# Two tokens in the two halves of the one-hot rows

## The chip, the core and the metric

The kernel runs on one core of a Trainium2 chip. The metric is the device time of the whole program in microseconds (us), taken as the median of several executions. Before the change it is 1927.19 us, from three runs between 1919.88 and 1936.14 us. One further execution was recorded by the hardware profiler; all rows below come from it.

The engines are called as in the profile: PE is TensorE's matrix multiply, PEld its weight load, DVE is VectorE, ACT is ScalarE, POOL is GpSimd and SP is SyncE, which issues DMAs.

## What is computed

The output is `x + A(xn) + B(xn)`, with `xn` the layer norm of x (2048 tokens, 512 wide).

- A is attention with 32 heads of width 16 that share one key and one value head, followed by an output projection.
- B is a mixture of 4096 tiny experts. For each of 32 heads a token has scores against 64 + 64 half keys; the two best of each give four candidate pairs, and the two best of those four are two experts with softmax gates. An expert is a row of `u` and a row of `v`: its contribution is `gate * gelu(xn . u) * v`. So a token uses 64 (head, choice) slots.

```
out = einsum("nhk,nhk,nhkd->nd", g, act, ve)     # g: gates, act: gelu(xn . u[e]), ve: v[e]
```

## The kernel before

The tokens are 16 tiles of 128, in four groups of 512. The kernel is one long list of 256 **attention steps** (`att_steps`), written out in order for every engine. A step issues, for TensorE, two score products, eight products with the values, two more score products (L327, L341, L327), and on ScalarE four exponentials of 128x1024 (L330). Behind these, in `fill`, each step pulls work for the expert part from a generator (`score_thread`). Every piece of it yields a cost (in units of about a microsecond; a 512-wide matmul counts `UNIT = 0.235`); `spent` adds these up, and step d of 256 pulls pieces until `spent` reaches a straight line that ends at `FILL = 948`, or until 4.0 units (`MOST`) are pulled in this step. So the costs that are yielded decide in which step a piece comes, and not how long it takes.

For the groups 0 and 1 (phases with `ph < NSP`) the experts' rows are gathered from HBM by indirect DMA on POOL (L976), and DVE forms a dot product (L988) and an update (L1023) for each of 512 gathered tiles. These are spread over the steps by `pos`, which advances per step by a number that depends on the stage (1.4 in the stage that the change touches, `dense_on[0] == 2`).

For the groups 2 and 3 the experts are computed **densely**: all 4096 rows of `u` are multiplied with the group (`pact`, L733), the result is multiplied with a dense matrix of gates (4096 experts by 512 tokens), and then by all of `v` (`pout`, L861). The change is in how that **matrix of gates** is made, once per dense group, so twice in the program:

1. `batch` writes for each token its 64 slots: two index numbers per slot (df1: 0 to 127, df2: 0 to 31, which together name one of 4096 experts), on POOL (L635, L638), and its gate, on DVE, as a float16 part and a remainder (L648, L649). The index is written twice, once for the gate's high part and once for its remainder, so a token has 128 numbers per array: rows 0 to 63 with the high gates, rows 64 to 127 with the remainders.
2. `spread` (L758) transposes the arrays on TensorE, so that the 128 rows lie on the partitions and the tokens along the row, and ScalarE copies each out of PSUM as float16 (L759).
3. `onehot(q)` builds, for 16 tokens, on DVE, `oa` (128 rows x 128 numbers x 16 tokens, 1 where the number is the row's index, L783), `ob` (128 x 32 x 16, the same for the second index, L785) and multiplies `ob` by the gates (L786). It is called two pieces ahead.
4. For each token one matmul `pg` (L815): `oa`'s 128x128 slice of this token is loaded as weights, `ob`'s 128x32 slice is streamed through. The sum over the 128 rows adds each slot's high part and remainder at its expert's place. Sixteen tokens fill one PSUM bank (128 x 512).
5. `copies` (L820) brings the bank to SBUF by two ScalarE copies of 128x256; every fourth piece, 64 tokens are written to HBM by SP's queue (L825, L827). The copies of a piece are issued before the next piece of the generator, or in the middle of the next attention step.

```
oa, ob = OH.pop(q)
p = xtile("pg")
for i in range(TB):
    nc.tensor.matmul(p[:, i * NB:(i + 1) * NB], oa[:, :, i], ob[:, :, i], start=True, stop=True)
...
yield 2.0
```

There are 32 such pieces (`NQ`) of 16 tokens (`TB`) in a dense group. `xtile` takes one of three PSUM banks that all short products share; the scores have four banks of their own, and L341's product one. The one-hot tiles come from a pool of eight tiles (`wk`) that the float32r halves of `u` and `v` use too.

## Time and profile before

| | us |
|---|---|
| median of 3 runs | 1927.19 |
| lowest and highest | 1919.88, 1936.14 |
| the profiled execution | 1931.19 |
| its span on the core | 1929.5 |
| PE busy | 1865.4 (97%) |
| DVE busy | 1633.0 (85%) |
| ACT busy | 1294.3 (67%) |
| POOL busy | 693.5 (36%) |

The span is the time from the first to the last instruction, and busy is the time in which an engine had at least one instruction in work. TensorE's clock is granted in stretches; the page gives it as a share of full speed, and its mean over the execution is 0.98. In the answers of the trace, "x32" is a count of instructions, "128*128" the rows and columns of the array that a matmul or weight load takes, and an arrow names what an engine waited for.

The two stretches with `pg` matmuls begin at 609 us and at 1417 us of the span.

### The profile page before, as it was taken

The numbers are of one execution on the slowest core, as the hardware profiler recorded it, in microseconds if no ns is written. First come the engines' busy times: TensorE is split into PE (matmuls) and PEld (weight loads), VectorE is DVE, ScalarE is ACT, GpSimd is POOL, SyncE is SP. The second block draws the span as 40 slices with busy tenths as digits, with TensorE's granted clock in tenths as the row PEclk, the third lists the DMA queues.
The fourth block names the chain that finished last, engine by engine and source line by source line (L and its number), as shares of the span: only waits on it lengthen the run. The fifth ranks groups of instructions, "written<-read, shape, count | busy, mean of one in ns | idle before, by whom it ended". The sixth has DMA issues, their size and how long they took to land.

```text
span 1929.5 us, 35007 instructions
## 1 busy us (share of the span) xinstructions
PE 1865.4 (97%) x10990; PEld 995.2 (52%) x10990; DVE 1633.0 (85%) x6381; ACT 1294.3 (67%) x1803; POOL 693.5 (36%) x920
## 2 busy tenths in 40 slices
PE   6879999999999999999999999999999999999998
PEld 4544444555555544555555454555555555555553
DVE  6626788889998976999999897899988879999994
ACT  3336666655557887877877555555578877888873
POOL 1202334334453213343444354344522124344430
PEclk9989999999999989999999999999999999999999
DMA  7856878887673668799889977877645778899882
GB/s 269 300 202 229 291 263 294 287 294 277 231 268 121 216 213 260 248 283 292 267 288 308 353 278 241 295 243 264 216 138 194 267 222 291 271 284 284 283 274 83
DMA packets 245724, 491.14 MB, mean 255 GB/s; under 512 B 93972, under 2 KB 106260, under 8 KB 245532
## 3 DMA queue, kind: packets, MB, share of 16 engines
q0 software_dynamic: 73728, 268.47, 41.4%
q1 hardware_dynamic: 170568, 219.56, 34.9%
q8 instruction: 88, 1.44, 0.3%
q10 hardware_dynamic: 1236, 0.82, 0.1%
q14 instruction: 104, 0.85, 0.1%
HBM read 427.41 MB, written 56.07 MB: 251 GB/s over the span
## 4 chain that ended last, share of the span: by engine, by line
PE 84%; DVE 3%; ACT 2%; issue 1%; DMA 1%; another core or an unknown queue 0%; SPq 0%; ACTq 0%; DVEq 0%
PE pv L341 23%; PE psc L531 18%; PE sc L327 17%; PE pact L733 10%; PE pout L861 9%; PE pg L815 2%; PE pwo L434 2%; ACT pt L330 2%; PE pw L487 2%; DVE oh L783 1%; DMA wk<-dw 1%; DVE xa L1023 1%; DMA wqt<-in_wqT_dram 0%; PE pwt L494 0%; PE pwl L409 0%
## 5 line engine op out<-in xcount | busy, mean ns | idle before, releaser
L330 ACT ACTIVATE pt<-sc 128x1024 f32<-128x1024 f32 x1024 | 994.4, 1026 | 459.2 <-PE sc L327 405.9
L976 POOL DMA_INDIRECT g<-in_uv_dram,idx x512 | 555.0, 1084 | 1009.5 <-DVE xa L1023 531.9
L341 PE MATMUL pv<-pt,vaug 128*32 128x512 f32 x4096 | 508.9, 615 | 0.0
L531 PE MATMUL psc<-wk,xt 128*128 128x512 f32 x1536 | 390.9, 402 | 6.6 <-DVE wk L497 3.5
L327 PE MATMUL sc<-qa,kaug 64*128 64x512 f32 x2048 | 387.0, 453 | 7.7 <-ACT pt L330 6.9
L1023 DVE SCALAR_TENSOR_TENSOR xa<-g,w,xa 128x512 f32<-128x512 f32 x512 | 371.5, 744 | 0.1
L988 DVE CUSTOM_DVE_ANT_0 g<-g,xa 128x512 f32<-128x512 f32 x512 | 335.2, 680 | 6.6 <-DMA g<-in_uv_dram,idx 6.6
L531 PEld LDWEIGHTS psc<-wk,xt 128*128 128x128 f32 x1536 | 279.4, 189 | 110.5 <-issue 40.3
L327 PEld LDWEIGHTS sc<-qa,kaug 64*128 64x128 f32 x2048 | 157.1, 187 | 326.1 <-ACT pt L330 194.3
L341 PEld LDWEIGHTS pv<-pt,vaug 128*32 128x32 f32 x4096 | 108.8, 111 | 255.7 <-issue 254.1
L546 DVE FIND_INDEX8 i<-m,psc 128x8 uint32<-128x64 f32 x1024 | 206.2, 220 | 0.0
L733 PE MATMUL pact<-xt,wk 128*128 128x512 f32 x768 | 196.0, 400 | 0.0
L861 PE MATMUL pout<-wk,wd 128*128 128x512 f32 x768 | 194.9, 402 | 0.2 <-DVE wd L919 0.2
L544 DVE MAX8 m<-psc 128x8 f32<-128x64 f32 x1024 | 146.1, 213 | 41.2 <-PE psc L531 40.0
L861 PEld LDWEIGHTS pout<-wk,wd 128*128 128x128 f32 x768 | 140.8, 188 | 47.4 <-issue 5.5
L733 PEld LDWEIGHTS pact<-xt,wk 128*128 128x128 f32 x768 | 139.4, 188 | 48.6 <-issue 17.9
L864 DVE TENSOR_TENSOR da<-da,pout 128x512 f32<-128x512 f32 x128 | 82.7, 678 | 10.1 <-PE pout L861 8.6
L698 DVE TENSOR_TENSOR wk<-rw,wk 128x512 fp32r<-128x512 f32 x128 | 84.7, 682 | 7.1 <-ACT wk L697 7.1
L783 DVE TENSOR_TENSOR oh<-oh 128x2048 f16<-128x2048 f16 x64 | 78.0, 1219 | 2.3 <-PE pg L815 1.7
L815 PEld LDWEIGHTS <-oh 128*128 128x128 f16 x1024 | 68.4, 163 | 13.6 <-issue 4.8
L815 PE MATMUL pg<-oh 128*128 128x32 f16 x1024 | 73.7, 246 | 0.8 <-DVE oh L786 0.7
L697 ACT CAST wk<-rw 128x512 fp32r<-128x512 f32 x128 | 74.0, 632 | 0.0
(159 smaller groups left out, 1356.4 us busy)
## 6 DMA issues: line engine op xcount, KB each, us to landing
wk<-dw SPq DMA_DIRECT2D x96, 512.0 KB
wqt<-in_wqT_dram SPq DMA_DIRECT2D x32, 512.0 KB
dw<-wk SPq DMA_DIRECT2D x32, 512.0 KB
rw<-in_ub_dram SPq DMA_DIRECT2D x64, 256.0 KB
rw<-in_vb_dram SPq DMA_DIRECT2D x64, 256.0 KB
gy<-dg SPq DMA_DIRECT2D x64, 256.0 KB
qa<-dqh SPq DMA_DIRECT2D x128, 64.0 KB
g<-in_uv_dram,idx POOLq DMA_INDIRECT x512
```

The lines of the kernel that those rows point to most:

```text
L327: nc.tensor.matmul(p[:, b, :], kaug[o:o + 64, kc * P:(kc + 1) * P], QA[u][o:o + 64, i, :], start=True, stop=True)
L330: nc.scalar.activation(pt, p, AF.Exp, scale=SCALE)
L341: nc.tensor.matmul(PV[u][32 * j:32 * j + 32, :], vaug[:, kc, :], pt[:, b, :], start=kc == 0, stop=kc == 15)
L531: nc.tensor.matmul(p, XT[k][:, a, j * P:(j + 1) * P], WC[n_][k][:, bb, :], start=n == 0, stop=n == 11)
L544: nc.vector.max(m8[:, jb, s, :], p[:, s * E:(s + 1) * E])
L546: nc.vector.max_index(i8[:, jb, s, :], m8[:, jb, s, :], p[:, s * E:(s + 1) * E])
L733: nc.tensor.matmul(p, us[:, a, k * P:(k + 1) * P], XT[k][:, c, :], start=n == 0, stop=n == 11)
L815: nc.tensor.matmul(p[:, i * NB:(i + 1) * NB], oa[:, :, i], ob[:, :, i], start=True, stop=True)
L861: nc.tensor.matmul(p, wd[0][:, a, j * P:(j + 1) * P], vs[:, c, :], start=n == 0, stop=n == 5)
L976: nc.gpsimd.indirect_dma_start(out=gt, out_offset=None, in_=uv, in_offset=bass.IndirectOffsetOnAxis(ap=IDX[ph, c, ti][:, s:s + 1], axis=0))
L988: nc.vector.tensor_tensor_reduce(u, u, XN[TPH * ph + ti], scale=1.0, scalar=0.0, op0=OP.mult, op1=OP.add, accum_out=a[:, i:i + 1])
L1023: nc.vector.scalar_tensor_tensor(acc, v, w[:, i:i + 1], acc, op0=OP.mult, op1=OP.add)
```

## The change

A one-hot tile now serves 32 tokens instead of 16: rows 0 to 63 hold the 64 slots of an even token, rows 64 to 127 those of the odd token behind it. A token then has 64 rows, so one matmul can no longer sum high parts and remainders; two matmuls of 64 rows each do it one behind the other into the same place (`start=r == 0, stop=r == 1`), with the same weights. `ob` comes in two versions, times high gates and times remainders.

What follows from it in the code:

- `batch` writes the indices once; the four arrays (df1, df2, high gates, remainders) are one tile of the pool `da` where they were three halves of two tiles.
- `spread` runs four times instead of three, and takes from each array and 128-token block the even and the odd tokens by two products with every second column of the identity (64 columns each), in place of a transpose of 128 columns. Its copy is 128x256 in place of 128x512.
- `onehot` is called one piece ahead instead of two; a piece has one `oa` for 32 tokens, one comparison for `ob` and two multiplications.
- `pg` goes to two PSUM banks per piece, one for the even tokens, one for the odd ones; four copies per piece put the tokens back in order, so they write every second element.
- A piece yields 3.6 instead of 2.0; there are 16 instead of 32 per group. `FILL` goes from 948 to 935. The loads that hang on piece numbers (`later_split` and what follows) are moved to the pieces with about the same tokens.

```diff
-FILL = 948.0
+FILL = 935.0
 ...
     def dense_tiles():
-        for _ in range(2):
-            da = big.tile([P, 2, D], F32, name="da", tag="da", bufs=2)
-            for i in range(2):
-                DT.append(da[:, i, :].rearrange("p (t r s) -> p t r s", t=GT, r=2))
+        da = big.tile([P, 4, GT, 64], F32, name="da", tag="da", bufs=2)
+        DT.extend(da[:, i] for i in range(4))
...
-        for r in range(2):
-            G_.tensor_add(df2[:, :, r, w], hi, ii[:, 1])
+        G_.tensor_add(df2[:, :, w], hi, ii[:, 1])
...
-            V.tensor_copy(dgt[:, :, 0, w], gh)
-            stt(dgt[:, :, 1, w], gg, GS, gh, op0=OP.mult, op1=OP.subtract)
+            V.tensor_copy(dgh[:, :, w], gh)
+            stt(dgl[:, :, w], gg, GS, gh, op0=OP.mult, op1=OP.subtract)
...
-        NQ = 512 // TB
+        NQ = 512 // (2 * TB)
...
             for j in range(GT):
-                nc.tensor.transpose(p[:, j * P:(j + 1) * P], DT[n][:, j].rearrange("p r s -> p (r s)"), ident)
-            nc.scalar.copy(tr[:, n, :], p)
+                for h in range(2):
+                    nc.tensor.matmul(p[64 * h:64 * h + 64, 64 * j:64 * j + 64], DT[n][:, j, :], ident[:, h::2],
+                                     start=True, stop=True)
+            nc.scalar.copy(tr[:, n, :], p[:, :256])
...
                 oa = kt(F16, (P, P, TB))
                 nc.vector.tensor_tensor(out=oa, in0=io, in1=bc(0, tb, P), op=OP.is_equal)
-                ob = obs[:, q % 3]
-                nc.vector.tensor_tensor(out=ob, in0=io[:, :NB, :], in1=bc(1, tb, NB), op=OP.is_equal)
-                nc.vector.tensor_mul(ob, ob, bc(2, tb, NB))
+                ob = obs[:, q % 2]
+                nc.vector.tensor_tensor(out=ob[:, 1], in0=io[:, :NB, :], in1=bc(1, tb, NB), op=OP.is_equal)
+                for i in range(2):
+                    nc.vector.tensor_mul(ob[:, i], ob[:, 1], bc(2 + i, tb, NB))
...
-            onehot(q + 2)
+            onehot(q + 1)
             oa, ob = OH.pop(q)
-            p = xtile("pg")
+            ps_ = [xtile("pg") for _ in range(2)]
             for i in range(TB):
-                nc.tensor.matmul(p[:, i * NB:(i + 1) * NB], oa[:, :, i], ob[:, :, i], start=True, stop=True)
+                for r in range(2):
+                    for h in range(2):
+                        o = slice(64 * h, 64 * h + 64)
+                        nc.tensor.matmul(ps_[h][:, i * NB:(i + 1) * NB], oa[o, :, i], ob[o, r, :, i],
+                                         start=r == 0, stop=r == 1)
...
-                for hb in range(2):
-                    nc.scalar.copy(st[hb][:, :, ql * TB:(ql + 1) * TB], pv_[:, 16 * hb:16 * hb + 16, :])
-                if ql == 3:
+                for h in range(2):
+                    pb = ps_[h].rearrange("p (t b) -> p b t", b=NB)
+                    for hb in range(2):
+                        to = st[hb][:, :, ql * 2 * TB:(ql + 1) * 2 * TB].rearrange("p b (t h) -> p b t h", h=2)
+                        nc.scalar.copy(to[:, :, :, h], pb[:, 16 * hb:16 * hb + 16, :])
+                if ql == 1:
...
-            yield 2.0
+            yield 3.6
```

More of the change, by code (lines that the diff above doesn't have):

```diff
@@ L623, in batch @@
             dense_tiles()
-        df1, df2, dgt = DT[:3]
+        df1, df2, dgh, dgl = DT
         ii = T("ii", F32, [P, 2, BT, 8])
@@ L633, in batch @@
         G_.tensor_scalar(hi, ii[:, 1], 32.0, -32.0, op0=OP.is_ge, op1=OP.mult)
-        for r in range(2):
-            G_.tensor_add(df2[:, :, r, w], hi, ii[:, 1])
+        G_.tensor_add(df2[:, :, w], hi, ii[:, 1])
         G_.tensor_scalar(hi, hi, -2.0, None, op0=OP.mult)
-        for r in range(2):
-            G_.tensor_add(df1[:, :, r, w], hi, ii[:, 0])
+        G_.tensor_add(df1[:, :, w], hi, ii[:, 0])
         def gates():
@@ L726, in dense @@
         yield 0.0
-        df1, df2, dgt = DT[:3]
         def activations(b, us, p):
@@ L757, in spread @@
             for j in range(GT):
-                nc.tensor.transpose(p[:, j * P:(j + 1) * P], DT[n][:, j].rearrange("p r s -> p (r s)"), ident)
-            nc.scalar.copy(tr[:, n, :], p)
+                for h in range(2):
+                    nc.tensor.matmul(p[64 * h:64 * h + 64, 64 * j:64 * j + 64], DT[n][:, j, :], ident[:, h::2],
+                                     start=True, stop=True)
+            nc.scalar.copy(tr[:, n, :], p[:, :256])
         io = kt(F16, (P, P, TB))
         nc.sync.dma_start(io, d_io)
-        tr = kt(F16, (P, 3, 512))
+        tr = kt(F16, (P, 4, 256))
         hh = late[0].tile([P, 2, 512], F32, name="gy", tag="gy", bufs=3)
@@ L772, in dense @@
             yield None
-        spread(2)
-        yield 0.45
+        for n in (2, 3):
+            spread(n)
+            yield 0.45
         dense_on[0] = 2
@@ L801, in load_totals, with copies @@
                     LIVE.add(t)
-        obs = kt(F16, (P, 3, NB, TB))
+        obs = kt(F16, (P, 2, 2, NB, TB))
         onehot(0)
         yield from rest_of_first
-        onehot(1)
         for q in range(NQ):
-            t0, ql = q // 4 * 64, q % 4
+            t0, ql = q // 2 * 64, q % 2
             if ql == 0:
                 st = [late[0].tile([P, 16, 64], F32, name="gst", tag="wd", bufs=4) for _ in range(2)]
-            onehot(q + 2)
+            onehot(q + 1)
             oa, ob = OH.pop(q)
-            p = xtile("pg")
+            ps_ = [xtile("pg") for _ in range(2)]
             for i in range(TB):
-                nc.tensor.matmul(p[:, i * NB:(i + 1) * NB], oa[:, :, i], ob[:, :, i], start=True, stop=True)
-            pv_ = p.rearrange("p (t b) -> p b t", b=NB)
-            def copies(pv_=pv_, st=st, ql=ql, t0=t0):
-                for hb in range(2):
-                    nc.scalar.copy(st[hb][:, :, ql * TB:(ql + 1) * TB], pv_[:, 16 * hb:16 * hb + 16, :])
-                if ql == 3:
+                for r in range(2):
[3 more added lines that the diff above has]
+                                         start=r == 0, stop=r == 1)
+            def copies(ps_=ps_, st=st, ql=ql, t0=t0):
+                for h in range(2):
[4 more added lines that the diff above has]
+                if ql == 1:
                     def part(b0, b1, st=st, t0=t0):
@@ L834, in dense @@
             POST.append((copies, lambda: None))
-            if q in (NQ - 16, NQ - 12):
-                later_split((NQ - 16, NQ - 12).index(q))
-            if q == NQ - 3:
+            if q in (NQ - 8, NQ - 6):
+                later_split((NQ - 8, NQ - 6).index(q))
+            if q == NQ - 2:
                 on_act(lambda: halves.__setitem__(2, half_split(2, 0)))
-            if q == NQ - 3:
+            if q == NQ - 2:
                 quiet[0] = 3
-            if q == NQ - 2:
+            if q == NQ - 1:
                 dense_on[0] = 3
@@ L845, in dense @@
                 later_split(2)
-            if q == NQ - 1:
                 later_split(3)
-            yield 2.0
+            yield 3.6
         held, ready, used = [], [], [0]
```

## The prediction

> **What bounds the kernel now.** First the page: which engine is full, and where along the span that is otherwise.

> ```profile
> PE 1865.4 (97%) x10990; PEld 995.2 (52%) x10990; DVE 1633.0 (85%) x6381; ACT 1294.3 (67%) x1803; POOL 693.5 (36%) x920
> ...
> PE   6879999999999999999999999999999999999998
> ...
> DVE  6626788889998976999999897899988879999994
> ...
> PEclk9989999999999989999999999999999999999999
> ...
> PE 84%; DVE 3%; ACT 2%; issue 1%; DMA 1%; another core or an unknown queue 0%; SPq 0%; ACTq 0%; DVEq 0%
> ```

> PE is full nearly everywhere and carries 84% of the chain that ended last; the kernel's time is a sum of PE work. DVE has slices that are as full. So the next view is by stretch: the two in which `pg` is made, then single attention steps of the first.

> ```profile
> 609.47:716.75 107.28, 105.84 (x951) 55.38 (x950) 97.50 (x201) 91.90 (x153) 21.48 (x18) 0.90 0.64 205
> 1417.71:1528.33 110.62, 105.18 (x964) 56.78 (x963) 99.94 (x203) 93.04 (x154) 26.33 (x23) 0.92 0.60 199
> ```

> ```profile
> 615.21:620.56 5.35, 5.35 (x60) 3.10 (x58) 5.21 (x14) 4.92 (x9) 0.00 (x0) 1.00 0.08 21
> ...
> 684.54:691.60 7.06, 7.06 (x60) 3.35 (x58) 6.38 (x14) 5.20 (x10) 1.15 (x1) 0.76 0.84 263
> ...
> 666.70:671.50 4.80, 4.62 (x43) 2.19 (x42) 4.70 (x11) 4.29 (x9) 1.95 (x2) 1.00 0.98 260
> ```

> The columns are: length, busy time of PE, PEld, DVE, ACT, POOL, granted clock, DMA share, GB/s. The two stretches take 107.28 + 110.62 = 217.9 us, 36 steps. A step with two pieces (32 tokens) takes 5.35 us, with PE at 5.35, DVE at 5.21 and ACT at 4.92: three engines are close together, PE ahead. The same step takes 7.06 us where the clock was 0.76. A step with one piece (16 tokens) takes 4.80 us.

> The low clock has a pattern, shown by windows of 3.41 us, the length of the clock's stretches here:

> ```profile
> 681.79:685.20 3.41, 3.41 (x40) 2.59 (x38) 3.38 (x7) 2.55 (x5) 2.13 (x2) 1.00 0.80 238
> 685.20:688.62 3.42, 3.42 (x18) 0.60 (x16) 3.32 (x10) 2.43 (x4) 1.15 (x1) 0.50 0.71 254
> 702.27:705.68 3.41, 3.41 (x46) 2.48 (x38) 2.37 (x6) 2.78 (x5) 2.01 (x2) 1.00 0.81 233
> 705.68:709.10 3.42, 3.42 (x27) 1.21 (x28) 3.39 (x9) 3.42 (x8) 0.91 (x1) 1.00 0.94 328
> ```

> A window that holds a whole burst of 32 `pg` (40 PE instructions) is followed by one at half clock; the third row holds such a burst too and is not. From the mean clocks 0.90 and 0.92 the stretches lose 0.10 x 107.28 + 0.08 x 110.62 = 19.6 us, and a cold window costs 7.06 - 5.35 = 1.71 us: some 11 to 12 of them.

> **The change, part by part.** *The matmuls.* What decides is the pace of `pg`:

> ```profile
> 646.62 2.13 PEld L815 LDWEIGHTS <-oh 128*128 128x128 f16 x32 [0.36 <-DVE xa L1023]
> ...
> 643.68 0.19 PEld L327 LDWEIGHTS sc<-qa,kaug 64*128 64x128 f32 x2 [0.61 <-ACT pt L330]
> 643.68 0.49 PE L327 MATMUL sc<-qa,kaug 64*128 64x512 f32 x2 [0.31 <-ACT pt L330]
> ...
> L327 PEld LDWEIGHTS sc<-qa,kaug x2048: 182/183/335, 140.2 to 1910.0; 64*128 64x128 f32 x187
> L327 PE MATMUL sc<-qa,kaug x2048: 383/492/793, 140.2 to 1910.3; 64*128 64x512 f32 x187
> ...
> L815 PEld LDWEIGHTS <-oh x1024: 141/166/182, 613.0 to 1528.1; 128*128 128x128 f16 x171
> ...
> 649.51 0.16 PEld L341 LDWEIGHTS pv<-pt,vaug 128*32 128x32 f32 x8 [0.36 <-issue]
> ```

> (Where a row has three durations, they are the least, the median and the greatest, in ns.) Thirty-two weight loads, each with its matmul, take 2.13 us, 66.6 ns a pair. The change doubles their number: 64 for 32 tokens. Each has 64 rows, and rows 0 to 63 and 64 to 127 alternate. The trace holds exactly this form: the scores (L327) use 64 rows, alternating, into two banks. Two of their loads together took 0.19 us where one takes 183 ns, two matmuls together 0.49 us where one takes 492 ns. So two halves of the array load and multiply at the same time, started within 10 ns. From that I take one pair of halves at 66.6 ns, 33.3 ns per matmul: 64 take 2.13 us again, the change in `pg` is **0**. The bounds: 33.3 ns, or no overlap, 66.6 ns, which would add 1024 x 66.6 ns = +68 us. I take the low end because the nearest rows, of the same shape of array, show two at the price of one. The instructions would then come at four per 66.6 ns, 17 ns each; the L341 row has eight loads in 0.16 us, so out of PE's own queue it can start that fast, in short runs.

> *Attention around them.* The built program has one piece of 32 tokens in each of 16 consecutive steps per group, where it had 14 steps of 32 and 4 of 16. So the 36 steps become 32; four steps' attention goes to other stages with as much other work as before, and costs PE there what it cost here. The yielded costs fall by 32 x 2.0 - 16 x 3.6 = 6.4 per group, less 0.45 for the fourth `spread`, 11.9 in all, and the line's end by 13, so the rest of the work keeps its steps nearly. What goes is the surplus of the 8 one-piece steps: 4.80 us against (5.35 - 2.13) + 1.07 = 4.29 us, 8 x 0.51 = **-4 us**.

> *DVE.* Its rows of the first stretch, with ACT's, and the waits of the `pg` loads over the whole span (microseconds, times):

> ```profile
> L783 DVE TENSOR_TENSOR oh<-oh 128x2048 f16<-128x2048 f16 x31 | 37.8, 1219 | 1.7 <-PE pg L815 1.7
> ...
> L820 ACT COPY gst<-pg 128x256 f32<-128x256 f32 x64 | 21.6, 411 | 0.2 <-PE pg L815 0.2
> ...
> L786 DVE TENSOR_TENSOR oh<-oh 128x512 f16<-128x512 f16 x32 | 13.6, 425 | 1.2
> L785 DVE TENSOR_TENSOR oh<-oh 128x512 f16<-128x512 f16 x31 | 12.9, 417 | 0.0
> ```

> ```profile
>   DVE oh L785: 3.3, 9
>   DVE oh L786: 2.5, 6
>   DVE xa L1023: 1.3, 4
>   DVE oh L783: 0.7, 2
> ```

> For 32 tokens DVE now does 2 x (1219 + 417 + 425) = 4122 ns and will do 1219 + 417 + 2 x 425 = 2486 ns: 1.64 us less, 52 us over 32 pieces. Nearly all of it lies beside PE and is worth nothing. What is worth something is PE's wait for the one-hot tiles, 3.3 + 2.5 + 0.7 + 1.3 = 7.8 us; the first piece of a group still waits, and part of each wait is PE's own switch, so **-5 us**, between 0 and -8. The call one piece ahead instead of two is covered: a piece is one step, its 2.5 us are issued ahead of the step's updates, and the 5.35 us of a step hide them; without that cover it would be 2.5 us a step. POOL's saved adds are nothing, as no wait names them.

> *ACT.* Copies per 32 tokens stay four of 128x256, 411 ns each by their row. That they write every second element is not in the trace; I take no difference, between 0 and +0.4 us each if the write takes twice as long, which beyond the 5.35 - 4.92 = 0.43 us of slack would add up to 1.2 us a step, 38 us. All four now stand behind each other between the second and third exponential, where two stood. By a step's rows (ACT 4.92 of 5.35) the round still closes; nothing.

> *PSUM.* Two of the three banks per piece, freed in the middle of the next step, as two pieces did before: nothing. *DMAs:* the same writes of 64 tokens, the same loads at the same tokens; SP's queue passes nothing new: nothing.

> *The transposes.*

> ```profile
> 1420.89 1.09 PE L758 MATMUL ptd<-ident,da 128*128 128x128 f32 x8
> 1423.30 0.66 PE L758 MATMUL ptd<-ident,da 128*128 128x128 f32 x4 [1.31 <-ACT oh L759]
> ```

> Eight take 1.09 us, 136 ns each, 24 in all 3.3 us. The 64 new ones have half the columns: at half the price 4.4 us, at the full one 8.7 us, and between halves of the array that overlap 2.2 us. I take +1 us, between -1 and +5. The wait of 1.31 us stays.

> *The switch of the array.* Behind the burst at 646.62 the loads end at 648.75, and the next score's load starts at 648.85; such a pause of about 0.1 us stands on either side of a burst. If it comes from going between 128 and 64 rows, it goes: 32 x 2 x 0.1 = -6 us; if not, 0. I take -2. [...]

> *Cold windows.* Bursts keep their length of 2.13 us and come once per step; I take the same 19.6 us: 0.

> Sum: 0 - 4 - 5 + 1 - 2 = **-10 us**. Against the profiled execution, 1931.19 us, that gives 1921; that execution is 4 us above the median of the runs shown, and from the median it gives 1917. I predict 1919 us. By 1%, 19 us, is about what a measurement of this kernel tells from no change; the forecast lies within it. Its own range is 1908 to 1931 us.

> **The rivals.**

> *No overlap (slower).* The two halves could take turns, since their weight loads come every 33 ns and no row shows float16 loads of 64 rows. Halving the rows does not halve a load: the 64-row load of the scores takes 183 ns, the 128-row float16 one 166 ns (medians). Then 64 matmuls take 4.26 us and a step 7.48 us: +68 us, and a burst longer than a window of 3.41 us leaves nearly every step a cold window: 32 x 1.71 = 55 us against 19.6, +35 at most. 1977 to 2022 us, about 1995. It decides from some 48 ns per matmul on, where 2048 x 15 ns make 30 us and the time is 1% above before. Against it: the rows of the scores.

> *PE is fed too slowly (slower).* The bursts now are never faster than 66.6 ns per load and matmul; if its sequencer can hand over no more than that, and a queue holds some 16 of them ready when a burst starts (my assumption; no row gives its depth), then of 64 the first 32 run at 33 ns, in the time in which 16 more arrive, and the last 32 at 66.6: 32 x 1.07 = +34 us, 1953 us. For it speaks that no longer run in the trace is faster. [...]

> *Locked cold windows (slower).* Four steps in a row from 677.45 to 705.59 us took about 7.06 us, close to two windows of 3.41 us: once a burst falls into a window, the next one falls there as well. So far the one-piece steps broke this. Without them all 32 could lock: 55 us against 19.6, 1919 + 35 = 1954 us.

> *No cold windows (faster).* If matmuls in both halves count as more work for whatever grants the clock, the 19.6 us go: 1899 us.

> *DVE never cost anything.* Its waits turn into ACT's, and it stays at 1924 to 1931 us; this lies in the forecast's range.

> **How the numbers follow.** Forecast with the last rival 0.53, no overlap 0.18, fed too slowly 0.11, locked 0.08, no cold windows 0.10. Range: from 1897, with the fast case, to 1965, with the two middle ones; left out is the case of no overlap, 0.18. Faster by over 1% (below 1908): 0.10 + 0.03 = 0.13. Slower by over 1% (above 1946): 0.18 + 0.08 of the fed one + 0.06 of the locked one = 0.32. Within: 0.55.

> **What would show it.** In the profile after, a burst of 64 weight loads of 64 rows takes 2.1 us if the forecast holds, 2.9 to 3.2 us if fed too slowly, 4.3 us without overlap. Steps of the stretch at full clock take 5.1 to 5.4 us, DVE falls to about 1580 us busy, and hardly a wait of `pg` for the one-hot tiles is left but the first of a group. The stretches' clock near 0.91 means that the cold windows are as before; near 0.76 that they are locked. The prediction is wrong if the burst is longer than 2.5 us, or if ACT's copies take over 0.6 us.

## The result, and the profile after

The changed kernel takes 1950.11 us (median of 11 runs, 1941.72 to 1956.99), the kernel before beside it 1928.37 us (11 runs): ratio **1.0108**, 95% interval 1.0085 to 1.0131. It is slower by 1.1%, 22 us. The forecast was 1919 us and "no change that can be told"; the time is 31 us above it, though inside the stated range of 1897 to 1965 us.

The same program was measured again on three chips, numbered 5, 6 and 10, always beside the kernel before; the record does not name the chip of the first measurement. Since the outcome depends on the chip, the table has each; everything below compares runs of one chip, or ratios. A "pause" is idle time of TensorE within a burst, the run of `pg` matmuls of one piece, for which the profile names no releaser.

| | ratio to before | interval | pauses in `pg` bursts |
|---|---|---|---|
| first measurement | 1.0108 | 1.0085 to 1.0131 | yes |
| `after_4` (chip 5) | 1.0103 | 1.0071 to 1.0135 | yes |
| `after_again` (chip 6) | 1.0035 | 1.0009 to 1.0060 | no |
| `after_3` (chip 10) | 1.0022 | 1.0000 to 1.0044 | no |

So there are two questions: why the kernel gained nothing anywhere, and what costs another 0.7 to 0.8% where the bursts pause. The page of the kernel after, with the groups of `pg` and the two queues of the kind "instruction":

```profile
PE 1868.2 (96%) x12118; PEld 998.4 (51%) x12118; DVE 1586.8 (81%) x6317; ACT 1294.8 (66%) x1805; POOL 679.0 (35%) x888
...
q8 instruction: 97, 1.59, 0.3%
...
q14 instruction: 102, 0.84, 0.1%
...
L816 PE MATMUL pg<-oh 64*128 64x32 f16 x2048 | 79.2, 245 | 6.8 <-issue 5.2
L816 PEld LDWEIGHTS <-oh 64*128 64x128 f16 x2048 | 72.0, 157 | 18.8 <-issue 16.5
```

The profiled execution took 1952.04 us, its span 1950.2 us. PE's busy time hardly moved (1865.4 to 1868.2 us) while the span grew by 20.7 us: PE is idle for 82.0 us where it was 64.1. DVE fell from 1633.0 to 1586.8 us, and the kernel is no shorter for it. In the last two rows the idle time ahead of the `pg` line has grown: PE's own was 0.8 us before, and its 6.8 us now are mostly "issue", a wait for nothing that the profile can name.

To see where the time is, the span is cut at the same attention steps in each kernel: steps 0 to 63, 64 to 87 (with the first `pg` stretch), 88 to 181, and 182 to 209 (with the second). Columns are as in the prediction: length, busy time of PE, PEld, DVE, ACT, POOL, clock, DMA share, GB/s. Before:

```profile
140.20:601.78 461.58, 451.89 (x2565) 232.95 (x2563) 391.29 (x2313) 287.90 (x368) 184.22 (x313) 0.99 0.76 260
601.78:751.56 149.78, 147.64 (x1167) 73.44 (x1166) 126.46 (x266) 123.66 (x197) 36.05 (x36) 0.93 0.67 214
751.56:1410.90 659.34, 655.66 (x3684) 357.26 (x3684) 597.66 (x2530) 445.92 (x592) 283.58 (x369) 1.00 0.83 273
1410.90:1591.46 180.56, 175.12 (x1333) 90.84 (x1333) 146.84 (x333) 144.98 (x224) 45.45 (x51) 0.94 0.64 204
```

After, first measurement:

```profile
139.39:603.20 463.81, 448.85 (x2554) 230.15 (x2552) 389.68 (x2282) 287.05 (x366) 181.13 (x291) 0.99 0.78 263
603.20:762.66 159.46, 153.41 (x1748) 79.56 (x1747) 103.38 (x257) 123.84 (x197) 35.53 (x42) 0.93 0.61 191
762.66:1422.77 660.11, 651.85 (x3662) 353.41 (x3663) 595.25 (x2485) 447.09 (x594) 276.01 (x356) 1.00 0.83 273
1422.77:1610.56 187.79, 180.05 (x1919) 96.14 (x1918) 129.13 (x353) 146.60 (x227) 43.18 (x48) 0.95 0.61 197
```

The four parts differ by +2.2, +9.7, +0.8 and +7.2 us, 19.9 of the 20.7 us. The parts with `pg` hold most of it. But look at the first and third row too: they lost 11 and 22 PE instructions (2565 to 2554, 3684 to 3662) and are yet a little longer. That other work went into the two `pg` parts.

### The profile page after: what moved, and what is told of

The parts are those of the page before. It is cut to its first block, busy times and chain, and to the rows that moved or that the text cites. A ratio compares the mean times of both kernels' runs of the same rounds, so it can differ in the third digit from the quotient of the medians.

```text
span 1950.2 us, 37163 instructions
## 1 busy us (share of the span) xinstructions
PE 1868.2 (96%) x12118; PEld 998.4 (51%) x12118; DVE 1586.8 (81%) x6317; ACT 1294.8 (66%) x1805; POOL 679.0 (35%) x888
## 2 busy tenths in 40 slices
PE   6879999999999999999999999999999999999998
## 3 DMA queue, kind: packets, MB, share of 16 engines
q8 instruction: 97, 1.59, 0.3%
## 4 chain that ended last, share of the span: by engine, by line
PE 81%; DVE 4%; ACT 4%; DMA 2%; issue 2%; another core or an unknown queue 0%; SPq 0%; ACTq 0%; DVEq 0%
PE pv L341 23%; PE psc L531 18%; PE sc L327 16%; PE pact L728 8%; PE pout L864 8%; PE pg L816 3%; ACT pt L330 2%; PE pwo L434 2%; PE pw L487 1%; DVE xa L1026 1%; DMA gy<-dg 1%; DVE g L991 1%; PE pwl L409 0%; DVE da L867 0%; PE pwt L494 0%
## 5 line engine op out<-in xcount | busy, mean ns | idle before, releaser
L330 ACT ACTIVATE pt<-sc 128x1024 f32<-128x1024 f32 x1024 | 994.8, 1028 | 473.0 <-PE sc L327 434.8
L341 PE MATMUL pv<-pt,vaug 128*32 128x512 f32 x4096 | 510.5, 616 | 0.0
L327 PE MATMUL sc<-qa,kaug 64*128 64x512 f32 x2048 | 390.0, 454 | 12.2 <-ACT pt L330 8.6
L327 PEld LDWEIGHTS sc<-qa,kaug 64*128 64x128 f32 x2048 | 160.3, 188 | 334.3 <-ACT pt L330 183.2
L341 PEld LDWEIGHTS pv<-pt,vaug 128*32 128x32 f32 x4096 | 109.0, 111 | 254.7 <-issue 253.0
L1014 DVE SCALAR_TENSOR_TENSOR w<-gth,ga 128x4 f32<-128x4 f32 x128 | 20.6, 161 | 107.9 <-ACT gth L1007 105.8
L816 PE MATMUL pg<-oh 64*128 64x32 f16 x2048 | 79.2, 245 | 6.8 <-issue 5.2
L816 PEld LDWEIGHTS <-oh 64*128 64x128 f16 x2048 | 72.0, 157 | 18.8 <-issue 16.5
```

What stands on the lines that cost most here:

```text
L327: nc.tensor.matmul(p[:, b, :], kaug[o:o + 64, kc * P:(kc + 1) * P], QA[u][o:o + 64, i, :], start=True, stop=True)
L330: nc.scalar.activation(pt, p, AF.Exp, scale=SCALE)
L341: nc.tensor.matmul(PV[u][32 * j:32 * j + 32, :], vaug[:, kc, :], pt[:, b, :], start=kc == 0, stop=kc == 15)
L816: nc.tensor.matmul(ps_[h][:, i * NB:(i + 1) * NB], oa[o, :, i], ob[o, r, :, i], start=r == 0, stop=r == 1)
```

## The experiments

### Does the pairing work?

The bursts of `pg` in the timeline of after:

```profile
1457.29 2.18 PEld L816 LDWEIGHTS <-oh 64*128 64x128 f16 x64 [0.28 <-issue]
```

64 loads in 2.18 us where 32 took 2.13 us: 34 ns per matmul, as forecast. To price the overlap, `no_pair` issues all 32 matmuls of the even tokens, then those of the odd ones; it stands on the version with two copies on DVE (below).

```diff
-            for i in range(TB):
-                for r in range(2):
-                    for h in range(2):
+            for h in range(2):
+                for i in range(TB):
+                    for r in range(2):
```

> The changed kernel with the odd tokens' copies on VectorE, and the matmuls of a piece in another order: first all 32 of rows 0 to 63, then all 32 of rows 64 to 127. Theory that the two halves of the array work at the same time only when they alternate: 66 ns instead of 33 per matmul, a burst of 4.3 us, and 32 x 2.1 = 68 us more than with the alternating order (1921.68), about 1990, with more half-clock windows up to 2020. Theory that a 64-row matmul costs 33 ns by itself: no difference.

Measured on chip 6: 2017.69 us, ratio 1.0498 (1.0434 to 1.0562), against 0.9995 with the overlap: 97 us. A burst in its timeline:

```profile
646.68 3.93 PEld L816 LDWEIGHTS <-oh 64*128 64x128 f16 x62 [0.27 <-DVE oh L785]
```

62 loads in 3.93 us, 63 ns each: the same instructions, not alternating, take twice the time. The rival without overlap had been priced at 1977 to 2022 us, and this run without overlap lies in that range.

Whether PE can be fed at that pace for long was the second rival. `twice` issues every matmul twice (the gates in its result are doubled).

```diff
-                for r in range(2):
+                for r in range(4):
...
-                                         start=r == 0, stop=r == 1)
+                                         start=r == 0, stop=r == 3)
```

> The version with copies on VectorE, with every matmul of a piece done twice (each gate is added twice, so the result holds the gates doubled): 128 weight loads and matmuls of 64 rows in one burst. Theory that PE's instructions come fast enough: the burst takes 128 x 33 ns = 4.3 us at one pace, and the kernel 68 us or more longer, 1990 to 2010. Theory that a long dense run outruns them: after the first 30 to 60 pairs the pace falls to 66 ns or pauses of 0.4 to 0.7 us appear, a burst takes 6 us or more, and the kernel takes over 2030.

Measured on chip 10: 2042.51 us (one run; 1924.28 for the version it is built on). A burst, and the 6.81 us that begin with it:

```profile
643.39 4.52 PE L816 MATMUL pg<-oh 64*128 64x32 f16 x128
```

```profile
643.39:650.20 6.81, 6.81 (x142) 5.21 (x144) 1.36 (x4) 3.52 (x4) 0.00 (x0) 0.74 0.01 2
```

128 in 4.52 us, 35 ns each and without a pause. So no limit of a queue that drains shows here. Of the 118 us, 32 x 2.2 us are longer bursts, 70 us; the rest goes with half clock (0.74 over these 6.81 us; 0.95 over the execution, where that of `copies_dve_2` has 0.986). The expectation had put over 2030 us with a pace that falls; the time came so, the fall of pace did not.

### The arrangement alone

`sched` is the kernel before with only the planner's numbers of the change. In its trace a group has two pieces in each of 15 steps and one piece in a step on either side, so it comes close to the arrangement of the changed kernel (32 tokens in each of 16 steps) without being the same.

```diff
-FILL = 948.0
+FILL = 935.0
...
-            yield 2.0
+            yield 1.8
```

> The kernel before with the arrangement of steps alone: a piece of 16 tokens yields 1.8 instead of 2.0 and the line ends at 935, so that two pieces (32 tokens) come in each of 16 consecutive steps, where the kernel before has 14 such steps and 4 of one piece. Theory that the new arrangement costs (equal steps lock the half-clock windows, and the four copies meet the exponentials): it takes about the 20 us of the change, 1.008 to 1.013 of before, and the clock of the two stretches falls below 0.90. Theory that the matmuls or their copies cost: within 5 us of before.

Measured on chip 6: 1938.67 us, ratio 1.0063 (1.0029 to 1.0096), between the two theories; the clock of its two `pg` stretches is 0.89 each, below 0.90 as the first had it. Without any new matmul the arrangement costs 12 us. Its four parts:

```profile
136.26:600.16 463.90, 449.31 (x2554) 229.78 (x2552) 389.56 (x2282) 287.08 (x366) 185.12 (x305) 0.99 0.78 263
600.16:755.92 155.76, 153.71 (x1190) 77.57 (x1190) 127.15 (x290) 125.33 (x197) 37.30 (x44) 0.92 0.62 198
755.92:1410.88 654.96, 649.21 (x3658) 352.24 (x3658) 594.33 (x2488) 446.29 (x593) 284.00 (x369) 1.00 0.84 275
1410.88:1596.55 185.67, 181.65 (x1353) 93.42 (x1352) 154.72 (x390) 146.14 (x227) 45.32 (x53) 0.94 0.65 206
```

Against before: +2.3, +6.0, -4.4, +5.1, together +9.0 us. The `pg` parts hold 23 and 20 more PE instructions, 512-wide matmuls of the stages around. What these take, by a row of the timeline of before:

```profile
598.16 3.70 PE L733 MATMUL pact<-xt,wk 128*128 128x512 f32 x15
```

247 ns each, so 5.7 and 4.9 us: all of the +6.0 and +5.1. Behind the first stretch the time comes back (26 fewer, 6.4 us, for 4.4 us). Ahead of it, it doesn't: 11 fewer, 2.7 us, and yet 2.3 us longer, because PE idles there for 14.6 us (463.90 less 449.31) where it idled for 9.7. That is 5 of the 9 us. What PE waits for in this part, in before and then in `sched`:

```profile
PE psc L531 <- DVE wk L497: 3.5, 4, 1.6
PE pwt L494 <- DVE i L546: 2.3, 1, 2.3
```

```profile
PE psc L531 <- DVE wk L497: 5.8, 6, 2.9
PE pwt L494 <- DVE i L546: 3.4, 2, 2.3
...
PE pwt L494 <- DVE wk L497: 1.6, 1, 1.6
```

The lower line puts the experts' scores (`psc`) and the weights made for them (`pwt`) into other steps, and there PE waits for DVE for 10.8 us instead of 5.8. It does so wherever the line ends at 935: PE idles for 14 to 17 us of this part in every other trace, after's included (463.81 less 448.85: 15.0 us), on all chips.

What the new one-hot rows bring can be told from three pairs of versions on chip 6, whose other runs come below. `sched` has the old rows and takes 1.0063 of before; with the new rows it is 0.9995 (`copies_dve`, two copies moved to DVE) or 1.0016 (`copies_split`, the copies in two pairs on ACT, much as `sched` has them). `sched_block`, old rows and four copies in a row, takes 1.0126; the changed kernel itself 1.0035. That is 13, 9 and 17 us, so **some 13 us**, each with an interval of 7 to 12 us to either side; in the first, moving two copies off ACT counts too. The arrangement that came with the rows takes it back.

### The four copies in a row

`copies_split` keeps the even tokens' two copies where they were and issues the odd tokens' two behind the fourth exponential. `copies_dve` gives the odd tokens' two to VectorE:

```diff
-                        nc.scalar.copy(to[:, :, :, h], pb[:, 16 * hb:16 * hb + 16, :])
+                        if h == 0:
+                            nc.scalar.copy(to[:, :, :, h], pb[:, 16 * hb:16 * hb + 16, :])
+                        else:
+                            nc.vector.tensor_copy(to[:, :, :, h], pb[:, 16 * hb:16 * hb + 16, :])
```

> The changed kernel with two of each piece's four copies (those of the odd tokens) moved from the middle of the next step to behind its fourth exponential, where the kernel before has the copies of its first piece. Theory that four copies in a row delay the exponentials and so PE: 5 to 12 us faster than the changed kernel, about 1940. Theory of feeding: no difference beyond 4 us.

> The changed kernel with the copies of the odd tokens on VectorE instead of ScalarE, so ScalarE does 0.8 us less per step where VectorE has 1.6 us of slack. Theory of ScalarE's order: 8 to 20 us faster than the changed kernel, 1930 to 1942. Theory of feeding: within 4 us of it.

The times expected of these two, and of `no_rem` below, count from the first measurement, 1950.11 us, and are too high: the runs came from chip 6, which shows no pauses. Repeats put the versions on one chip:

> The changed kernel once more, for a second profile. If the pauses inside bursts and the half-clock windows belong to it, and not to one execution, there are again ten or more pauses of over 0.2 us inside bursts and a clock of 0.89 to 0.93 in the two stretches, and 1940 to 1957 us.

> The changed kernel, timed on one chip together with the two versions of its copies below. It has taken 1950.11 (with 11 and 8 pauses inside the bursts of its two stretches) and 1931.72 (with 2 and 2). If the pauses come with the chip, this run shows either all of them and about 1945 to 1955, or none and 1925 to 1935.

> The version with two of four copies behind the fourth exponential, beside the changed kernel on the same chip. Theory of ScalarE's order: 5 to 10 us faster than it, 0.3 to 0.5%. If the order of the copies isn't what costs: within 3 us.

> The version with the odd tokens' copies on VectorE, beside the changed kernel on the same chip. Theory of ScalarE's order and load: 7 to 13 us faster than the changed kernel, and so 0 to 5 us faster than the kernel before. If neither costs: within 3 us of the changed kernel.

| ratio to before | all four on ACT | split | two on DVE |
|---|---|---|---|
| chip 6 | 1.0035 | 1.0016 | 0.9995 |
| chip 10 | 1.0022 | 1.0006 | 0.9993 |

Each has an interval of about 0.002 to either side, so the split alone is not clear of noise on one chip. The order is the same on both: with two on DVE 4 to 8 us less, with the split 2 to 4 us less. On chip 10 that is less than the 7 to 13 and 5 to 10 us expected. Where it goes is in the timeline of after:

```profile
1461.84 1.23 ACT L824 COPY gst<-pg 128x256 f32<-128x256 f32 x4
1461.92 0.74 PE L327 MATMUL sc<-qa,kaug 64*128 64x512 f32 x4
...
1462.90 2.93 ACT L330 ACTIVATE pt<-sc 128x1024 f32<-128x1024 f32 x3
...
1464.05 0.49 PE L327 MATMUL sc<-qa,kaug 64*128 64x512 f32 x2 [1.39 <-ACT pt L330]
```

The scores at 1461.92 are soon done, but ACT is busy with the four copies until the third exponential can start at 1462.90; the next scores need its bank and PE stands for 1.39 us. This step is an extreme: it is the one step of the second stretch without a piece (16 pieces lie in 17 steps there), so no burst stands ahead of the scores at 1464.05. Where the burst fills that time the wait is smaller. A second place is the banks, in `after_again`:

```profile
654.32 0.59 ACT L349 COPY e<-pv 128x512 f32<-128x512 f32 x1
654.76 0.26 PE L816 MATMUL pg<-oh 64*128 64x32 f16 x1
654.80 1.26 ACT L824 COPY gst<-pg 128x256 f32<-128x256 f32 x4
655.52 2.21 PE L816 MATMUL pg<-oh 64*128 64x32 f16 x62 [0.50 <-ACT gst L824]
```

At the end of a unit another copy stands ahead of the four, the next burst has begun with its free bank, and its second matmul waits for the first copies. That comes twice in a stretch. What the copies cost over both stretches, by the `pg` parts of `after_3` and then of `copies_dve_2` (chip 10):

```profile
603.86:753.02 149.16, 145.67 (x1748) 77.12 (x1748) 103.25 (x257) 124.42 (x198) 35.48 (x42) 0.97 0.64 205
...
1411.22:1596.49 185.27, 179.48 (x1918) 95.90 (x1918) 128.94 (x353) 146.62 (x227) 43.20 (x48) 0.94 0.62 198
```

```profile
602.84:749.72 146.88, 144.31 (x1749) 76.71 (x1748) 113.81 (x289) 116.26 (x166) 33.88 (x42) 0.97 0.65 208
...
1405.67:1583.01 177.34, 173.56 (x1917) 94.29 (x1916) 140.04 (x385) 138.20 (x195) 41.04 (x48) 0.97 0.65 207
```

2.3 and 7.9 us in these two executions; that of `after_3` was 8 us slower than the median of its runs, so this is more than the copies cost on average. PE's idle time (length less busy time) makes 0.9 and 2.0 us of it. Most of the second is clock: 0.06 x 185 less 0.03 x 177 is 5.8 us. That the copies bring the half clock about is not shown.

The reverse, on the old one-hot rows: `sched_block` holds the two pieces' copies until four stand together in the middle of the next step.

```diff
     def run_scores(until=None, key=None):
         while (until is not None and spent[0] < until) or (key is not None and key not in IDX):
-            posts()
+            if len(POST) > 1:
+                posts()
```

> The kernel with the arrangement of steps alone (two pieces of 16 tokens in each of 16 steps, one-hot rows as before), but with the four copies of a step's two pieces one behind the other in the middle of the next step, as the changed kernel has them. Theory that four copies in a row delay the exponentials: 8 to 20 us slower than the arrangement alone (1938.67), so 1947 to 1959. Theory that the paired 64-row matmuls are what costs in the changed kernel: within 4 us of the arrangement alone.

1947.79 us, ratio 1.0126 (1.0067 to 1.0184), against 1.0063 for `sched`: +9 to 12 us. It has four runs, and the two intervals overlap. So four copies in a row cost 4 to 12 us with the new rows and, less surely, with the old ones.

### Fewer matmuls

`no_rem` leaves out the remainders' matmuls, so the gates keep their float16 parts alone; `no_rem_dve` leaves out their multiplication too and has two copies on DVE.

```diff
-                for r in range(2):
+                for r in range(1):
...
-                                         start=r == 0, stop=r == 1)
+                                         start=True, stop=True)
```

> The changed kernel without the remainder matmuls (the low parts of the gates are left out): 32 weight loads and matmuls of 64 rows per piece instead of 64, in bursts of 1.07 us. Theory that PE is fed too slowly in long dense runs: the pauses inside bursts (8.6 + 7.9 us of waits of the loads with no releaser) go, and with 1.07 us less in each of 32 pieces (34 us) the time falls by 40 to 50 us against the changed kernel, to about 1900 to 1910. Theory that ScalarE's order sets the steps: the pauses for exponentials stay or grow and the time falls by under 25 us, to 1925 to 1935.

> The changed kernel without the remainder matmuls and without the multiplication that feeds them (the low parts of the gates are left out), and with the odd tokens' copies on VectorE. Without the remainders alone it took 1918.63, with the copies on VectorE alone 1921.68. Theory that ScalarE bounds the steps once the bursts are short: ScalarE's 0.8 us less per step are worth 10 to 25 us here, 1894 to 1909. Theory that another engine or the feeding of PE bounds them: within 5 us of 1918.

Chip 6: 1918.63 us, 0.9969 (0.9952 to 0.9986), and 1910.76 us, 0.9933 (0.9907 to 0.9959). Half of the matmuls less, 32 x 1.1 = 35 us of PE, are worth 13 us against `after_again` (1.0035), and 12 us where the copies are out of the way (0.9933 against 0.9995). Much of the rest turns into PE's wait for the exponentials. In the waits of PE in the first `pg` part, of `no_rem` and of `after_again`:

```profile
PE sc L327 <- ACT pt L330: 7.8, 21, 0.4
```

```profile
PE sc L327 <- ACT pt L330: 1.3, 4, 0.4
```

Once the burst is short, PE waits for an exponential 21 times instead of 4. In the second part it is 10.3 us instead of 3.2, so some 14 of the 22 us that are missing are this wait; the other 8 are not accounted for. So a burst of half the length would bring 12 to 13 us here, as long as nothing else changes. `no_rem_dve` is 8 us faster than `no_rem`, less than the 10 to 25 expected if ScalarE alone bounds the steps.

### The pauses

In the first measurement bursts break off. One of them in its timeline, PE only, and then the same piece in `after_4`, the changed kernel again, on chip 5:

```profile
671.13 1.54 PE L816 MATMUL pg<-oh 64*128 64x32 f16 x38
...
673.09 0.32 PE L816 MATMUL pg<-oh 64*128 64x32 f16 x3 [0.41 <-issue]
...
673.81 0.95 PE L816 MATMUL pg<-oh 64*128 64x32 f16 x23 [0.41 <-issue]
```

```profile
671.51 1.54 PE L816 MATMUL pg<-oh 64*128 64x32 f16 x36
...
673.48 0.31 PE L816 MATMUL pg<-oh 64*128 64x32 f16 x3 [0.42 <-issue]
...
674.23 1.02 PE L816 MATMUL pg<-oh 64*128 64x32 f16 x25 [0.44 <-issue]
```

38 matmuls at full pace, then 3, then the rest, each time some 0.65 us from one start to the next; no semaphore is waited for. With `after_4` two versions ran on the same chip:

> The changed kernel itself, once more. Two theories of the 0.6 to 0.9% by which the first measurement (ratio 1.0108) lies above the two repeats (1.0035 and 1.0022). If the pauses of about 0.7 us inside the pg bursts belong to the chip or to where its memory put the code, they can come back here: some 10 to 20 of them in the trace, half-clock time in the two stretches above 40 us and a ratio of 1.007 to 1.013. If they were an accident of one measurement, there are at most 4 pauses, all of them waits for a bank, half-clock time of 25 to 32 us and a ratio of 1.001 to 1.005.

> The odd tokens' two copies on VectorE, on the same chip as the repeat of the changed kernel. Copies theory: 3 to 10 us below that repeat (a ratio to the kernel before of 0.997 to 1.001), because no score product waits behind four copies. If the repeat shows pauses inside bursts, they come here too if the chip causes them (ratio 1.003 to 1.009), and not if the four copies do (0.997 to 1.001).

> The odd tokens' two copies behind the fourth exponential, same chip. Copies theory: 2 to 6 us below the repeat of the changed kernel, ratio 0.999 to 1.003. If the chip causes pauses inside bursts, the ratio is 1.004 to 1.010.

Measured: 1.0103, 1.0065 (1.0037 to 1.0094) and 1.0065 (1.0040 to 1.0090). The copies still cost 0.4%, but every version is 0.5 to 0.8% above itself on chips 6 and 10. The idle time of the `pg` weight loads with no releaser, in `after_4` and in `after_3`:

```profile
  issue: 20.8, 53
```

```profile
  issue: 9.4, 27
```

With two copies on DVE it is 17.0 us on chip 5 against 6.3 on chip 10: 11 us more on chip 5, whatever the copies do. On chips 6, 8 and 10 the bursts hold no pause but waits for a bank or a one-hot tile. Where they fall, with pieces and matmuls counted from 0: in the first measurement in pieces 5, 8, 11, 13, 21, 24 and 26 of the 32, always from matmul 36 on; in `after_4` in the same pieces but the last, in `copies_dve_3` and `copies_split_3` in six and five of them, mostly within a few matmuls of the same place. So they belong to places in the program and come only on some chips. They would fit a supply of instructions that can't follow, which is a guess: the burst uses them up at 17 ns each (34 ns for a load and its matmul), twice the rate of the bursts before (66.6 ns).

But the bursts are not all. In just these four traces (after, `after_4`, `copies_dve_3`, `copies_split_3`), and in that of the kernel before, ScalarE starts some exponentials late: their scores are done and it is free, and yet it starts 0.3 us to 3.9 us later. One of them in after, at attention step 140, and one in before:

```profile
1131.85 0.73 PE L327 MATMUL sc<-qa,kaug 64*128 64x512 f32 x4
1135.04 1.02 ACT L330 ACTIVATE pt<-sc 128x1024 f32<-128x1024 f32 x1 [5.62 <-remote]
```

```profile
1336.96 0.73 PE L327 MATMUL sc<-qa,kaug 64*128 64x512 f32 x4
1339.71 1.94 ACT L330 ACTIVATE pt<-sc 128x1024 f32<-128x1024 f32 x2 [2.62 <-remote]
```

The exponential starts 3.19 and 2.75 us behind the first of its scores; in `after_3`, at the same step 140, it is 0.60 us. Each of the five traces has 7 to 12 such delays, 8 to 12 us together, and no trace of chips 6, 8 and 10 has one. In the changed kernel they come at the same steps each time (7, 22, 50, 59, 140 and 178 in all four). ScalarE runs only about one instruction per microsecond (1805 in the span), so a high rate of instructions is not needed for such a delay, and the kernel before has them too, only no pause inside its bursts. What the pauses cost is less sure than that they come: in after PE's idle time of this kind in the `pg` line is 5.2 us, and the rest of the 13 to 16 us between the chips is not divided up. Three runs were to tell the supply of instructions from another cause:

```diff
+    pad = xtile("pad")
+    for _ in range(96):
+        nc.tensor.matmul(pad[:, :32], ident, ident[:, :32], start=True, stop=True)
     transpose_group(0)
```

> The changed kernel with 96 additional small matmuls ahead of the first transposes, whose result nobody reads: about 10 us more at the start, and every later TensorE instruction 192 places further in the program. On a chip that shows pauses without a releaser in the bursts of pieces 5, 8, 11, 13, 21, 24 and 26: if they belong to places in the program (supply of instructions), they move to other pieces, about one piece earlier each, since a piece with its attention step is about as many instructions. If they belong to the time or to what else runs in these steps (a load, a copy), they stay in the same pieces. On a chip without pauses it tells nothing but the price of the additional matmuls.

> Every pg matmul twice (the gates in the result are doubled), the odd copies on VectorE. On a chip with pauses, supply theory: bursts of 128 use up instructions for 4.5 us at the high rate, so pauses come in more of the pieces, 40 or more in all and over 25 us. If the pauses come from something else in these steps, about 16 as before.

> The same instructions in an order in which the halves of the array can't overlap: 66 ns per matmul, half the rate of instructions. On a chip with pauses, supply theory: no pauses but the waits for a bank, since the supply has twice the time. If something else in the steps causes them, the same 8 to 12 us of pauses.

They ran on chip 8, which shows no pauses, and tell nothing of them: 1958.6, 2048.64 and 2018.26 us beside 1922.17 us before (one run each). The additional matmuls of `shift` cost about 30 us at the start instead of 10. **Open**: that the pauses are a lack of instructions is argued, not shown, and why one chip has them and another not is unknown. In after the two queues of the kind "instruction" moved 1.59 MB in 97 packets (q8) and 0.84 MB in 102 (q14), in before 1.44 MB in 88 and 0.85 MB in 104; no run here shows an engine that has run out of instructions.

## Why the prediction was wrong, point by point

It forecast no change that can be told, and took 1% as the least that can be; the measurement told 1.1% with an interval of 0.23% to either side. Its own signs did not point to the loss: a burst without a pause took 2.2 us (wrong was to be over 2.5), a copy 0.43 us (over 0.6). Three terms were put at nothing or at a gain and cost time: the arrangement, ACT's four copies, and, on the chip of the first measurement, the pauses.

- **The matmuls, 0.** Right: 64 loads in 2.18 us against 32 in 2.13.
- **DVE, -5 us.** Right about the waits, 7.8 us before. In after, over the whole span, by the idle time of the loads ahead of the `pg` line, these are left (and 0.3 us of a third):

```profile
  DVE xa L1026: 1.1, 4
  DVE oh L785: 0.6, 2
```

- **The transposes, +1 us, and the switch, -2 us.** Right in size, the first by luck: its 24 old products were those of both groups, its 64 new ones those of one. The 64 products of a group have a busy time of 2.3 us where 12 had 1.7, so +1.2 us for both groups. A step with the whole burst at full clock, in `after_3`:

```profile
641.68:646.91 5.23, 5.23 (x95) 3.19 (x92) 1.56 (x6) 4.86 (x10) 0.00 (x0) 1.00 0.94 277
```

  5.23 us against 5.35: 0.12 us per step, about 4 us in all, from one step of each kernel; that it comes from the switch is not shown. The -2 was chosen between 0 and -6, and the -6 rests on pauses of about 0.1 us, such as from 648.75 to 648.85 us behind a burst of before; no run shows that going between 128 and 64 rows causes them, nor a switch within the waits for the one-hot tiles.
- **Attention around them, -4 us.** This is the first step that failed: "four steps' attention goes to other stages with as much other work as before, and costs PE there what it cost here", and "the rest of the work keeps its steps nearly". `sched` shows +12 us in place of -4. Lowering the line by what the pieces yield less moved 11 matmuls out of a part in which PE then waited 5 us more for DVE, and more matmuls into the `pg` parts. (The 16 steps are consecutive in the first stretch only; the second has 17, one of them without a piece.)
- **ACT, nothing.** The second step that failed: "By a step's rows (ACT 4.92 of 5.35) the round still closes". The mean load was right and beside the point: four copies in a row keep ACT busy for 1.23 us between two exponentials, and the next scores wait behind them. With two of them on DVE the kernel takes 4 to 9 us less, on three chips. That each writes every second element costs next to nothing (430 against 411 ns).
- **PSUM and DMAs, nothing.** Nearly so: the two waits for a bank in a stretch (2.6 us in all in `after_3`), and no wait for a transfer in the `pg` line.
- **Cold windows, 0.** Too cautious for the pairing. From the clocks of the `pg` parts, before loses 0.07 x 150 + 0.06 x 181 = 21 us, `copies_dve_2` 0.03 x 147 + 0.03 x 177 = 10 us. By these figures a part of what the new rows bring is this; the first measurement, with its pauses, kept the 21. The rival of locked windows did not come, not with the old rows either: `sched` loses 0.08 x 156 + 0.06 x 186 = 24 us, 3 more than before, where 55 had been its price.
- **The rival "fed too slowly"** came to +34 us from a queue of 16, an assumption that no run shows, and a supply of one load and matmul per 66.6 ns; in `twice` the pace does not fall (128 in 4.52 us, 35 ns each). Something like it comes with the pauses: 13 to 16 us on some chips (1.0103 and 1.0108 against 1.0022 and 1.0035), and the first measurement had it. The forecast had put this at nothing, and beside the 16 us of the arrangement (+12 for -4) it is the largest part of the 31 us by which it missed. This is the third step that failed; its cause stays open.

So the sum on chips 6 and 10 reads: some 13 us gained by the rows, 12 lost by the arrangement (both measured on chip 6 alone), 4 to 8 by the copies; ratio 1.002 to 1.004. On the first chip what comes with the pauses is added. No version with the whole computation beat the kernel before: two copies on DVE give 0.9993 to 0.9995 without pauses, 1.0065 with them.

## What to carry to other kernels

A slack in the mean of an engine's step says nothing of a block in the middle of its chain: ask what waits for the instruction behind the block. When a change comes with new planner costs, run the old work in the new arrangement first; here that alone was as large as the gain. And measure on several chips before a difference of less than 1% is believed: here one program took 1.0022 to 1.0108 of the other.

## What the runs showed of the hardware that was not expected

```profile
625.58:628.99 3.41, 3.41 (x44) 2.68 (x40) 3.38 (x10) 2.48 (x4) 0.00 (x0) 1.00 0.01 2
628.99:632.40 3.41, 3.41 (x20) 0.59 (x16) 3.38 (x7) 2.48 (x4) 0.47 (x1) 0.50 0.84 308
```

```profile
638.22:641.63 3.41, 3.41 (x75) 2.38 (x69) 3.27 (x10) 3.41 (x7) 0.00 (x0) 1.00 1.04 382
641.63:645.05 3.42, 3.42 (x40) 1.38 (x38) 0.16 (x2) 3.05 (x7) 0.00 (x0) 1.00 1.02 288
```

- Bursts that filled a whole window (4.52 us against 3.41) were the worst: in `twice` all 18 windows that held at least 92 matmuls of one burst were followed by half clock.
- Pauses of about 0.65 us from start to start, tied to places in the program, on one chip out of four named here and in the first measurement; in the same traces, and in that of the kernel before, ScalarE starts 7 to 12 exponentials 0.3 to 3.9 us late.
